# Gate and value products of a token-mixing MLP on one core: exchanging the stationary and the streamed operand

## The chip, the cores and the metric

One core of a Trainium2 chip runs the whole program in one launch. The metric is the device time in microseconds (us). Engines are named as in the profile: PE is TensorE, split into PE (the matmul streams) and PEld (the loads of the stationary operand), DVE is VectorE, ACT is ScalarE, POOL is GpSimd, SP is SyncE, whose queue issues the DMAs here.

## The reference, cut to what matters

Attention over 8 batches, 8 heads, 512 local and 32 global tokens makes x with 8 × 544 rows (tokens) of 512 columns. A two-layer MLP with a gate follows:

```python
xk = mu_k * x + (1.0 - mu_k) * x_prev
xr = mu_r * x + (1.0 - mu_r) * x_prev
k = np.maximum(xk @ w_k, 0.0)
v = k * k @ w_v
r = 1.0 / (1.0 + np.exp(-(xr @ w_r)))
return (r * v).astype(np.float32)
```

w_k is 512 × 1024, w_v 1024 × 512, w_r 512 × 512. The *keys* are `xk @ w_k`, the *gate* is r, the *values* are v. The output has 512 columns, called e below.

## The kernel before

**Tiling.** Tokens are worked in groups of 256 (`TOK`): two for each batch, and one for all global tokens, 17 in all. Features lie on the 128 partitions and tokens along the row. Each operand is split into a high part in the rounded 4-byte format that PE streams fast (`F32R`) and a low part, the rest, in the same format. A product is three matmuls: high × high, high × low, low × high (`products`, L615; `matmul`, L159, is the helper that every matmul passes through, so that its line in the profile is L160; transposes are L163).

**Gate** (`gates`, L706, and for the first batch `step_gates`, L1147, with `step_tanh`, L1154). For each 128-column block of w_r, 4 contraction blocks × 3 matmuls are made: the weight block is stationary, 256 tokens stream. Two such blocks fill one bank of PSUM. A token group has 4 blocks, so 48 matmuls of 256 columns. ACT then takes the tanh out of the bank (L717, L1158), and after the second bank one more ACT instruction maps the whole gate tile to 0.5 + 0.5·tanh (L719, L1160).

**Values.** The four token groups of batches 0 and 1 use plain products (`values`, L722, and `step_values`, L1162): 8 contraction blocks × 3 × 4 blocks = 96 matmuls of 256 columns for each group. DVE multiplies a finished bank into the gate tile and the result is stored (L731, `write` L741). Batches 2 to 7 and the global tokens use seven (or, for the global tokens, four) products of sums of blocks instead of eight (`Keys.product`, L820): the stationary operand is a 128-column piece of a sum of weight blocks (`left`, loaded from `scratch`), the streamed one is a sum of key blocks for 256 tokens (`right`, split by ACT and by DVE or POOL at L787 and L788). Halves of the outputs are summed by DVE and multiplied into the gate by POOL (`write`, L745), then stored.

**Output.** The gate tile is `[P, NC, TOK]`: features on partitions, blocks of e, then tokens; a half of the columns e is a contiguous half of a partition's row. The outputs are laid out as `(C, P, B, SL)` and `(C, P, B * SG)`, e first, and put in order on the host. A store (L916, L921) writes 1 KB runs of tokens.

**Order.** PE runs strictly in the order of the source (`in_line`, L149, chains every matmul to the one before). ACT, DVE and POOL keep the order of the source too. SP does so for the first stretch. That stretch (up to about 123 us) is written out by hand in `FIRST` (L66): steps such as `W.0.1` (gate, token group 0, part 1), `V.1.0` (values), `L.12` (low part of weight chunk 12 made by POOL). The eight chunks of w_v are loaded 12 to 19, chunk 12, that of contraction block 0, last. Later batches alternate attention steps and MLP steps by a pattern (`BATCH`, L1365); each `yield` in `gates` and `values` ends one MLP step. At `FILL_AT` (L1364) four small transposes are inserted into one gate.

```python
def products(out, w_h, w_l, cols, x_h, x_l, n):
    for i in range(n):
        matmul(out, w_h[:, i, cols], x_h(i), start=(i == 0), stop=False)
        matmul(out, w_h[:, i, cols], x_l(i), start=False, stop=False)
        matmul(out, w_l[:, i, cols], x_h(i), start=False, stop=(i == n - 1))
```

The first operand after `out` is the stationary one, the second is streamed.

Of the kernel before, what the change touches and what calls it, by code (L numbers as in the profile page):

```python
# [10 lines left out]
F32 = mybir.dt.float32  # L11
# [9 lines left out]
P = 128  # L21
D = 64
SG = 32
SL = 512
# [66 lines left out]
def local_global_attention_then_rwkv_ffn(  # L91
# [49 lines left out]
    def psum(tag):  # L141
        n = turn[tag] = turn.get(tag, -1) + 1
        pool = use[tag][n % len(use[tag])]
        return pool.tile([P, 512], F32, tag="ps", name=f"ps_{tag}")
# [473 lines left out]
            matmul(out, w_h[:, i, cols], x_l(i), start=False, stop=False)  # L618
            matmul(out, w_l[:, i, cols], x_h(i), start=False, stop=(i == n - 1))

    class Tokens:


# [81 lines left out]

        def gates(self, pool=None, fill_at=None):  # L706

            pool = pool or gatep
            self.gate = pool.tile([P, NC, TOK], F32, tag="gate", name="gate")
            for e0 in range(0, NC, 2):  # L710
                rp = psum("m").rearrange("p (j n) -> p j n", j=2)
                for j in range(2):
                    if (j, e0) == fill_at:
                        fill_narrow(rp[:, j], 4)
                    products(rp[:, j], wr_h, wr_l, slice((e0 + j) * P, (e0 + j + 1) * P),
                             lambda c: self.xr_h[:, c], lambda c: self.xr_l[:, c], NC)
                Tokens.square = nc.scalar.activation(self.gate[:, e0:e0 + 2], rp, AF.Tanh, scale=0.5)  # L717
                if e0 + 2 == NC:
                    nc.scalar.activation(self.gate, self.gate, AF.Copy, scale=0.5, bias=0.5)  # L719
                yield  # L720

        def values(self):  # L722
            for e0 in range(0, NC, 2):
                vp = psum("m").rearrange("p (j n) -> p j n", j=2)
                for j in range(2):
                    products(vp[:, j], wv_h, wv_l, slice((e0 + j) * P, (e0 + j + 1) * P),
                             lambda f: self.kk_h[f], lambda f: self.kk_l[f], NF)
                    if j == 0:
                        yield
                o = self.gate[:, e0:e0 + 2]  # L730
                nc.vector.tensor_mul(o, vp, o)  # L731
                self.store(slice(e0, e0 + 2), o)
                yield

        def write_one(self, e, v):

            o = self.gate[:, e]
            nc.vector.tensor_mul(o, v, o)
            self.store(slice(e, e + 1), self.gate[:, e:e + 1])

        def write(self, half, v):  # L741

            es = slice(2 * half, 2 * half + 2)
            o = self.gate[:, es]
            (nc.vector if v.tensor.name.startswith("ps_") else nc.gpsimd).tensor_mul(o, v, o)  # L745
            self.store(es, o)

    class Keys:

# [70 lines left out]
        def product(self, out, b, fresh=True, apart=False, between=None):  # L820
            right = self.parts.pop(b)
            steps = [(i, j) for i in range(HC) for j in range(2)]
            if between:
                steps.sort(key=lambda x: x[1])
            for i, j in steps:
                a, (b_h, b_l) = left[i // 2], right[i // 2]
                a_h, a_l = (a[:, i % 2, x, j * P:(j + 1) * P] for x in range(2))
                for n, (w, x) in enumerate(((a_h, b_h), (a_h, b_l), (a_l, b_h))):
                    matmul(
                        out[j] if apart else out[:, j], w, x[:, i % 2],  # L830
                        start=fresh and (i, n) == (0, 0) and (apart or j == 0),
                        stop=(i, n) == (HC - 1, 2), skip_group_check=True,
                    )
# [58 lines left out]
        def values_of_one(self):  # L892

            t, = self.tokens
            X, Y = self.bank(), [self.bank()[:, 0] for _ in range(2)]
            parts = [self.parts[f"B{b}1"] for b in (1, 2)]

            def product(out, b, **how):
                self.parts["end"] = parts[b]
                self.product(out, "end", fresh=not b, **how)  # L900
            product(X, 0)
            yield
            product(Y, 0, apart=True)
            yield
            product(X, 1)
            t.write(0, X)
            yield
            product(Y, 1, apart=True, between=lambda j: t.write_one(2 + j, Y[j]))
            yield


    def local_tokens(b, half, xT):
        at = half * TOK

        def store(es, o):
            nc.sync.dma_start(out=out_l[es, :, b, at:at + TOK].rearrange("e p n -> p e n"), in_=o)  # L916
        return Tokens(lambda c: xT[c][:, 1 + at:1 + at + TOK], lambda c: xT[c][:, at:at + TOK], lambda a: a, store)

    def global_tokens():
        def store(es, o):  # L920
            nc.sync.dma_start(out=out_g[es].rearrange("e p n -> p e n"), in_=o)  # L921
# [222 lines left out]
        kh, kl = squares_of(t, f)  # L1144
        nc.vector.tensor_sub(kl, banks["K", t, f], kh.bitcast(F32))

    def step_gates(t, e):  # L1147
        rp = banks["W", t, e] = psum("m").rearrange("p (j n) -> p j n", j=2)
        x_h, x_l = first[int(t)].part("r")
        for j in range(2):  # L1150
            at = (2 * int(e) + j) * P
            products(rp[:, j], wr_h, wr_l, slice(at, at + P), lambda c: x_h[:, c], lambda c: x_l[:, c], NC)

    def step_tanh(t, e):  # L1154
        t_, e0 = first[int(t)], 2 * int(e)
        if e0 == 0:
            t_.gate = gatep.tile([P, NC, TOK], F32, tag="gate", name="gate")
        nc.scalar.activation(t_.gate[:, e0:e0 + 2], banks["W", t, e], AF.Tanh, scale=0.5)  # L1158
        if e0 + 2 == NC:
            nc.scalar.activation(t_.gate, t_.gate, AF.Copy, scale=0.5, bias=0.5)  # L1160

    def step_values(e, j):  # L1162
        if j == "0":
            banks["V", e] = psum("m").rearrange("p (j n) -> p j n", j=2)
        at = (2 * int(e) + int(j)) * P
        products(banks["V", e][:, int(j)], wv_h, wv_l, slice(at, at + P),
                 lambda f: first[0].kk_h[f], lambda f: first[0].kk_l[f], NF)

    STEPS = {
        "@": step_load,  # L1170
# [31 lines left out]
        "W": step_gates,  # L1202
        "w": step_tanh,
        "V": step_values,
        "v": lambda e: first[0].write(int(e), banks["V", e]),
    }

    by_hand = ExitStack()
# [247 lines left out]
```

## Time and profile before

| | us |
|---|---|
| device time, median of 3 runs (lowest to highest) | 630.81 (630.70 to 631.17) |
| span of the profiled execution, first to last instruction | 628.5 |
| PE busy | 620.1 (99%) |
| PEld busy | 590.7 (94%) |
| DVE, ACT, POOL busy | 440.0, 379.7, 340.1 |

The page gives the profiled execution its span alone; the median of the runs is 2.3 us above that span. Matmuls are pipelined: a record opens before the array is free, so the pace of a run of matmuls is read from the distance between starts, or from a long run's length over its count, not from the duration of one. The chain of work that ended last is followed back from the last instruction, at each step to what released it; a stretch of it that lies on PE is one in which PE waited for nobody.

### The profile page before, as it was taken

The page shows a single profiled execution, that of the slowest core. Times are in us where ns is not written, and L with a number is a line of the kernel's source. Part 1 is how long each engine was busy: PE and PEld are TensorE (multiplying, and loading weights), DVE is VectorE, ACT ScalarE, POOL GpSimd, SP SyncE. Part 2 cuts the span into 40 slices and gives each one's busy share as a digit, 9 for nine tenths or more (in the row PEclk, how much of TensorE's full clock was granted, in tenths as well). Part 3 has the DMA queues.
Part 4 walks back from the last instruction along what each step waited for, and adds up shares of the span by engine and source line. Part 5 has one row for each costly group of instructions (what it writes and reads, how often), then busy time and mean ns, then how long its engine had stood idle before and what let it go on. Part 6 is the DMA issues. An engine that isn't in the chain of part 4 may idle for free.

```text
span 628.5 us, 20469 instructions
## 1 busy us (share of the span) xinstructions
PE 620.1 (99%) x8356; PEld 590.7 (94%) x8356; DVE 440.0 (70%) x1227; ACT 379.7 (60%) x1147; POOL 340.1 (54%) x310
## 2 busy tenths in 40 slices
PE   8999999999999999999999999999999999999997
PEld 4689999999999999999999999999999999999997
DVE  7999983758888487676695677676696657345960
ACT  6899967164383768565857657665847744433531
POOL 8786455536846245846276535846275534543660
PEclk9999999999999999999999999999999999999999
DMA  8955562457383546276463928276463834377684
GB/s 337 408 197 217 193 224 82 169 183 273 118 305 131 201 139 236 60 269 235 158 248 108 378 75 335 88 267 228 162 243 104 299 117 137 105 222 246 200 261 142
DMA packets 43278, 127.29 MB, mean 203 GB/s; under 512 B 3760, under 2 KB 20656, under 8 KB 43184
## 3 DMA queue, kind: packets, MB, share of 16 engines
q1 hardware_dynamic: 43184, 125.98, 56.1%
q8 instruction: 66, 1.08, 0.7%
q14 instruction: 28, 0.23, 0.1%
HBM read 108.66 MB, written 17.30 MB: 200 GB/s over the span
## 4 chain that ended last, share of the span: by engine, by line
PE 85%; DVE 5%; DMA 3%; POOL 3%; ACT 2%; issue 1%; DVEq 0%; POOLq 0%; ACTq 0%
PE ps_m L160 65%; PE ps_s L160 13%; PE ps_t L163 4%; PE ps_t L160 2%; DMA w<-w_v 2%; ACT Pt L417 1%; PE ps_s L163 1%; DMA raw_qk<-qk 1%; POOL wv_l L271 1%; DVE a L299 1%; DVE diff L664 1%; POOL w L252 1%; POOL Pt L428 0%; DVE diff L659 0%; DVE xfull L664 0%
## 5 line engine op out<-in xcount | busy, mean ns | idle before, releaser
L160 PE MATMUL ps_m<-xkh,wk_h 128*128 128x256 f32 x544 | 154.1, 283 | 0.0
L160 PE MATMUL ps_m<-xkl,wk_h 128*128 128x256 f32 x544 | 150.5, 277 | 0.0
L160 PE MATMUL ps_m<-xkh,wk_l 128*128 128x256 f32 x544 | 150.5, 277 | 0.0
L160 PE MATMUL ps_m<-bh,a 128*128 128x256 f32 x736 | 131.7, 278 | 0.0
L428 POOL TENSOR_TENSOR Pt<-Pt,ssum 128x512 f32<-128x512 f32 x64 | 69.4, 1088 | 81.0 <-ACT Pt L417 38.9
L160 PEld LDWEIGHTS ps_m<-bh,a 128*128 128x128 f32 x736 | 113.1, 188 | 0.0
L417 ACT ACTIVATE Pt<-Pt,m 128x128 f32<-128x128 f32 x256 | 99.5, 395 | 14.4 <-DVE m L410 14.4
L160 PEld LDWEIGHTS ps_m<-xkh,wk_h 128*128 128x128 f32 x544 | 102.2, 188 | 3.7 <-issue 1.2
L160 PEld LDWEIGHTS ps_m<-xkh,wk_l 128*128 128x128 f32 x544 | 102.3, 188 | 0.0
L160 PEld LDWEIGHTS ps_m<-xkl,wk_h 128*128 128x128 f32 x544 | 102.2, 188 | 0.0
L160 PE MATMUL ps_m<-bl,a 128*128 128x256 f32 x368 | 101.7, 276 | 0.0
L160 PE MATMUL ps_m<-xrh,wr_h 128*128 128x256 f32 x272 | 76.7, 282 | 0.0
L702 ACT ACTIVATE relu<-ps_m 128x512 f32<-128x512 f32 x52 | 30.9, 595 | 74.3 <-PE ps_m L160 69.0
L669 POOL TENSOR_TENSOR xkl<-xfull,xkh 128x512 fp32r<-128x512 f32 x30 | 40.2, 1339 | 65.8 <-DVE ssum L361 33.6
L160 PE MATMUL ps_m<-xrl,wr_h 128*128 128x256 f32 x272 | 75.2, 277 | 0.0
L160 PE MATMUL ps_m<-xrh,wr_l 128*128 128x256 f32 x272 | 75.2, 276 | 0.0
L410 DVE CUSTOM_DVE_ANT_0 Pt<-ps_s,masks 128x128 f32<-128x128 f32 x256 | 55.9, 285 | 24.2 <-PE ps_s L160 24.2
L160 PEld LDWEIGHTS ps_m<-bl,a 128*128 128x128 f32 x368 | 69.2, 188 | 0.0
L669 POOL TENSOR_TENSOR xrl<-diff,xrh 128x512 fp32r<-128x512 f32 x30 | 41.5, 1383 | 41.8 <-DVE xrh L668 26.7
L788 DVE TENSOR_TENSOR bl<-B,bh 128x512 fp32r<-128x512 f32 x41 | 40.1, 992 | 27.6 <-ACT bh L787 27.4
L788 POOL TENSOR_TENSOR bl<-B,bh 128x512 fp32r<-128x512 f32 x35 | 47.8, 1387 | 19.1 <-ACT bh L787 11.4
L664 DVE SCALAR_TENSOR_TENSOR diff<-diff,mu_r_sb,xT 128x256 f32<-128x256 f32 x56 | 57.2, 1061 | 0.0
(154 smaller groups left out, 1477.3 us busy)
## 6 DMA issues: line engine op xcount, KB each, us to landing
a<-scratch SPq DMA_DIRECT2D x92, 512.0 KB, 4.8
raw_v<-v SPq DMA_DIRECT2D x32, 896.0 KB, 8.6
raw_qk<-qk SPq DMA_DIRECT2D x32, 628.0 KB, 5.0
out_l<-gate SPq DMA_DIRECT2D x32, 256.0 KB, 2.2
w<-w_k SPq DMA_DIRECT2D x8, 512.0 KB, 12.9
w<-w_v SPq DMA_DIRECT2D x8, 512.0 KB, 4.0
w<-w_r SPq DMA_DIRECT2D x4, 512.0 KB, 3.6
scratch<-wv_h SPq DMA_DIRECT2D x8, 256.0 KB, 2.7
```

The source lines that it names most:

```text
L160: return in_line(nc.tensor.matmul(*a, **kw))
L163: return in_line(nc.tensor.transpose(*a, **kw))
L252: nc.gpsimd.tensor_scalar(word(n, F32, 1), word(n, F32, 1), REBIAS, 1.0, op0=ALU.mult, op1=ALU.mult)
L271: nc.gpsimd.tensor_sub(part_of_weights(n, "l"), word(n, F32, 0), part_of_weights(n, "h").bitcast(F32))
L299: nc.vector.tensor_sub(s.bitcast(F32R), s, hs.bitcast(F32))
L410: nc.vector.tensor_tensor_reduce(out=self.Pt[:, i], in0=self.place(t, n, h), in1=masks[:, 2 * self.slots[t][1] + n], op0=ALU.add, op1=ALU. ...
L417: nc.scalar.activation(self.Pt[:, i], self.Pt[:, i], AF.Exp, bias=self.low_x[:, i:i + 1], scale=-1.0, accum_out=self.ssum[:, i:i + 1],)
L428: nc.gpsimd.tensor_mul(self.Pt[:, some], self.Pt[:, some], inv.unsqueeze(2).to_broadcast([P, 4, W]))
L664: nc.vector.scalar_tensor_tensor(self.shape(xf[:, j]), self.shape(d[:, j]), mu[:, c0 + j:c0 + j + 1], self.prev(c0 + j), op0=ALU.mult, op1 ...
L669: nc.gpsimd.tensor_sub(lo[:, both], xf, hi[:, both].bitcast(F32))
L702: nc.scalar.activation(rk, kp, AF.Relu)
L788: (by or (nc.vector if b[0] == "B" else nc.gpsimd)).tensor_sub(l, val, h.bitcast(F32))
```

## The change

Gate and plain value products put a block of 128 tokens in as the stationary operand and stream 512 weight columns past it. The blocked value products of batches 2 to 7 exchange their operands too and stay 256 columns wide. The result has tokens on partitions, so the gate tile is `[P, 2, NC * P]` (128 tokens, two token blocks, 512 columns e) and the outputs are `(B, SL, C * P)` and `(B * SG, C * P)`; a half of the columns e is now two pieces of 256 in a partition's row.

```diff
+    def by_tokens(out, x_h, x_l, j, w_h, w_l, part, n):
+        rows = slice(j * P, (j + 1) * P)
+        for i in part:
+            matmul(out, x_h(i)[:, rows], w_h[:, i], start=(i == 0), stop=False)
+            matmul(out, x_l(i)[:, rows], w_h[:, i], start=False, stop=False)
+            matmul(out, x_h(i)[:, rows], w_l[:, i], start=False, stop=(i == n - 1))
...
         def gates(self, pool=None, fill_at=None):
-            self.gate = pool.tile([P, NC, TOK], F32, tag="gate", name="gate")
-            for e0 in range(0, NC, 2):
-                rp = psum("m").rearrange("p (j n) -> p j n", j=2)
-                for j in range(2):
-                    if (j, e0) == fill_at:
-                        fill_narrow(rp[:, j], 4)
-                    products(rp[:, j], wr_h, wr_l, slice((e0 + j) * P, (e0 + j + 1) * P),
-                             lambda c: self.xr_h[:, c], lambda c: self.xr_l[:, c], NC)
-                Tokens.square = nc.scalar.activation(self.gate[:, e0:e0 + 2], rp, AF.Tanh, scale=0.5)
-                if e0 + 2 == NC:
+            self.new_gate(pool or gatep)
+            for j in range(2):
+                rp = psum("m")
+                if j == fill_at:
+                    fill_narrow(rp, 4)
+                self.gate_of(j, rp)
+                Tokens.square = nc.scalar.activation(self.gate[:, j], rp, AF.Tanh, scale=0.5)
+                if j:
                     nc.scalar.activation(self.gate, self.gate, AF.Copy, scale=0.5, bias=0.5)
                 yield
...
+        def new_gate(self, pool):
+            self.gate = pool.tile([P, 2, NC * P], F32, tag="gate", name="gate")
+        def gate_of(self, j, bank):
+            by_tokens(bank, lambda c: self.xr_h[:, c], lambda c: self.xr_l[:, c], j, wr_h, wr_l, range(NC), NC)
+        def values_part(self, j, half, bank):
+            part = range(half * NF // 2, (half + 1) * NF // 2)
+            by_tokens(bank, lambda f: self.kk_h[f], lambda f: self.kk_l[f], j, wv_h, wv_l, part, NF)
         def values(self):
...
+            for j in range(2):
+                vp = psum("m")
+                self.values_part(j, 0, vp)
                 yield
+                self.values_part(j, 1, vp)
+                self.write_rows(j, vp)
+                yield
+        def write_rows(self, j, v, es=slice(0, NC * P)):
+            o = self.gate[:, j, es]
             nc.vector.tensor_mul(o, v, o)
+            self.store(slice(j, j + 1), es, self.gate[:, j:j + 1, es])
         def write(self, half, v):
-            es = slice(2 * half, 2 * half + 2)
-            o = self.gate[:, es]
+            es = slice(half * TOK, (half + 1) * TOK)
+            o = self.gate[:, :, es]
             (nc.vector if v.tensor.name.startswith("ps_") else nc.gpsimd).tensor_mul(o, v, o)
-            self.store(es, o)
+            self.store(slice(0, 2), es, o)
...
                 a, (b_h, b_l) = left[i // 2], right[i // 2]
-                a_h, a_l = (a[:, i % 2, x, j * P:(j + 1) * P] for x in range(2))
-                for n, (w, x) in enumerate(((a_h, b_h), (a_h, b_l), (a_l, b_h))):
+                a_h, a_l = (a[:, i % 2, x] for x in range(2))
+                rows = slice(j * P, (j + 1) * P)
+                for n, (x, w) in enumerate(((b_h, a_h), (b_l, a_h), (b_h, a_l))):
                     matmul(
-                        out[j] if apart else out[:, j], w, x[:, i % 2],
+                        out[j] if apart else out[:, j], x[:, i % 2, rows], w,
...
-            product(Y, 1, apart=True, between=lambda j: t.write_one(2 + j, Y[j]))
+            product(Y, 1, apart=True, between=lambda j: t.write_rows(j, Y[j], slice(TOK, 2 * TOK)))
...
-            nc.sync.dma_start(out=out_l[es, :, b, at:at + TOK].rearrange("e p n -> p e n"), in_=o)
+            nc.sync.dma_start(out=out_l[b, at:at + TOK].rearrange("(j p) e -> p j e", p=P)[:, js, es], in_=o)
...
-    FILL_AT = {(B - 2, 1): (1, 0)}
+    FILL_AT = {(B - 2, 1): 0}
...
-    outs = {"out_l": (C, P, B, SL), "out_g": (C, P, B * SG)}
+    outs = {"out_l": (B, SL, C * P), "out_g": (B * SG, C * P)}
```

`step_gates`, `step_tanh` and `step_values` of the first stretch are rewritten to the same calls; the text of `FIRST` is unchanged, so that `V.1.0` now means token block 1, contraction blocks 0 to 3.

## Rows read from the trace of the kernel before

**Rows 1.** The page: span, busy time of each engine.
```profile
span 628.5 us, 20469 instructions
PE 620.1 (99%) x8356; PEld 590.7 (94%) x8356; DVE 440.0 (70%) x1227; ACT 379.7 (60%) x1147; POOL 340.1 (54%) x310
```
**Rows 2.** Chain that ended last, 523 us to the end: start us, us, what, count.
```profile
523.21 102.03 PE ps_m L160 x900
```
**Rows 3.** Busy time of PE, PEld, DVE, ACT, POOL in two stretches, then clock and DMA.
```profile
141.70:171.60 29.90, 29.64 (x371) 29.02 (x370) 25.73 (x43) 10.88 (x28) 22.18 (x19) 1.00 0.57 201
...
220.00:523.00 303.00, 303.00 (x4247) 293.61 (x4247) 213.04 (x603) 197.26 (x589) 163.88 (x127) 1.00 0.55 198
```
**Rows 4.** Groups by line and shape, PE and PEld: shape, count, busy us, mean ns, idle before.
```profile
L160 PE MATMUL ps_m<-bh,a 128*128 128x256 f32 x736 | 131.7, 278 | 0.0
L160 PE MATMUL ps_m<-xrh,wr_h 128*128 128x256 f32 x272 | 76.7, 282 | 0.0
L160 PE MATMUL ps_m<-kkh,wv_h 128*128 128x256 f32 x128 | 36.8, 287 | 0.0
...
L160 PEld LDWEIGHTS ps_m<-xrh,wr_h 128*128 128x128 f32 x272 | 51.1, 188 | 1.1
L160 PEld LDWEIGHTS ps_m<-xT,diag 128*128 128x128 f32 x32 | 5.7, 189 | 0.9 <-ACT xT L611 0.2
```
**Rows 5.** Chain that ended last, 87 to 117 us.
```profile
87.77 6.38 DMA w<-w_v
...
99.38 10.94 PE ps_m L160 x94
...
110.76 2.83 PE ps_m L160 x24
...
114.03 2.74 PE ps_m L160 x24
```
**Rows 6.** PE in order of time at 99 and 171 us: waits in brackets.
```profile
99.38 0.39 PE L160 MATMUL ps_m<-kkh,wv_l 128*128 128x256 f32 x1 [0.39 <-POOL wv_l L271]
...
171.60 0.62 PE L160 MATMUL ps_s<-raw_qk 128*64 128x480 f32 x2 [0.26 <-DVE m L410]
```
**Rows 7.** Chain that ended last, 143 to 171 us.
```profile
143.05 0.44 DVE kkh L682
...
169.50 1.11 DVE kkl L683
```
**Rows 8.** Chain that ended last, 213 to 221 us.
```profile
213.34 0.61 ACT relu L702
...
219.96 0.63 PE ps_t L163 x4
```
**Rows 9.** Matmuls with the high part of w_r in two stretches: PE busy us, count.
```profile
141.50:171.60 30.10, 5.49 (x32) 1.00 0.57 202
...
219.90:628.50 408.60, 70.20 (x400) 1.00 0.55 195
```
**Rows 10.** PEld in order of time, fp32 loads (xT, diag): first and last of three.
```profile
26.90 0.19 PEld L160 LDWEIGHTS ps_m<-xT,diag 128*128 128x128 f32 x1
...
27.33 0.19 PEld L160 LDWEIGHTS ps_m<-xT,diag 128*128 128x128 f32 x1
```
**Rows 11.** PE in order of time, fp32 matmuls of 256 columns (xT, diag) at 26 us.
```profile
26.36 0.48 PE L160 MATMUL ps_m<-xT,diag 128*128 128x256 f32 x1
26.68 0.38 PE L160 MATMUL ps_m<-xT,diag 128*128 128x256 f32 x1
```
**Rows 12.** The page's DMA issues: stores, KB each, median us to landing.
```profile
out_l<-gate SPq DMA_DIRECT2D x32, 256.0 KB, 2.2
```
**Rows 13.** POOL and DVE in order of time, multiplications into the gate tile.
```profile
289.04 1.67 POOL L745 TENSOR_TENSOR gate<-sum,gate 128x512 f32<-128x512 f32 x1 [0.15 <-DVE sum L879]
295.37 1.67 POOL L745 TENSOR_TENSOR gate<-sum,gate 128x512 f32<-128x512 f32 x1 [0.44 <-DVE sum L888]
622.60 0.69 DVE L745 TENSOR_TENSOR gate<-ps_m,gate 128x512 f32<-128x512 f32 x1 [12.02 <-issue]
```

More of the change, by code (lines that the diff above doesn't have):

```diff
@@ L706, in gates @@
         def gates(self, pool=None, fill_at=None):
-            pool = pool or gatep
-            self.gate = pool.tile([P, NC, TOK], F32, tag="gate", name="gate")
-            for e0 in range(0, NC, 2):
-                rp = psum("m").rearrange("p (j n) -> p j n", j=2)
-                for j in range(2):
-                    if (j, e0) == fill_at:
-                        fill_narrow(rp[:, j], 4)
-                    products(rp[:, j], wr_h, wr_l, slice((e0 + j) * P, (e0 + j + 1) * P),
-                             lambda c: self.xr_h[:, c], lambda c: self.xr_l[:, c], NC)
-                Tokens.square = nc.scalar.activation(self.gate[:, e0:e0 + 2], rp, AF.Tanh, scale=0.5)
-                if e0 + 2 == NC:
+            self.new_gate(pool or gatep)
@@ L719, in gates @@
+            for j in range(2):
[5 more added lines that the diff above has]
+                if j:
                     nc.scalar.activation(self.gate, self.gate, AF.Copy, scale=0.5, bias=0.5)
                 yield
-        def values(self):
[L723 to L732, printed above, removed]
-                yield
@@ L735, in write_one @@
-        def write_one(self, e, v):
-            o = self.gate[:, e]
+        def new_gate(self, pool):
[5 more added lines that the diff above has]
+            by_tokens(bank, lambda f: self.kk_h[f], lambda f: self.kk_l[f], j, wv_h, wv_l, part, NF)
@@ L738, in write_one @@
+        def values(self):
+            for j in range(2):
+                vp = psum("m")
+                self.values_part(j, 0, vp)
+                yield
+                self.values_part(j, 1, vp)
[3 more added lines that the diff above has]
+            o = self.gate[:, j, es]
             nc.vector.tensor_mul(o, v, o)
-            self.store(slice(e, e + 1), self.gate[:, e:e + 1])
+            self.store(slice(j, j + 1), es, self.gate[:, j:j + 1, es])
@@ L913, in local_tokens, with store @@
         at = half * TOK
-        def store(es, o):
-            nc.sync.dma_start(out=out_l[es, :, b, at:at + TOK].rearrange("e p n -> p e n"), in_=o)
+        def store(js, es, o):
+            nc.sync.dma_start(out=out_l[b, at:at + TOK].rearrange("(j p) e -> p j e", p=P)[:, js, es], in_=o)
         return Tokens(lambda c: xT[c][:, 1 + at:1 + at + TOK], lambda c: xT[c][:, at:at + TOK], lambda a: a, store)
     def global_tokens():
-        def store(es, o):
-            nc.sync.dma_start(out=out_g[es].rearrange("e p n -> p e n"), in_=o)
+        def store(js, es, o):
+            nc.sync.dma_start(out=out_g.rearrange("(j p) e -> p j e", p=P)[:, js, es], in_=o)
         return Tokens(lambda c: xg_all[:, c, :, 1:SG + 1], lambda c: xg_all[:, c, :, 0:SG],
@@ L1145, in step_squares_low, with step_gates, step_tanh, step_values @@
         nc.vector.tensor_sub(kl, banks["K", t, f], kh.bitcast(F32))
[L1147 to L1159, printed above, removed]
-            nc.scalar.activation(t_.gate, t_.gate, AF.Copy, scale=0.5, bias=0.5)
[L1162 to L1167, printed above, removed]
+    def step_gates(t, j):
+        banks["W", t, j] = psum("m")
+        first[int(t)].gate_of(int(j), banks["W", t, j])
+    def step_tanh(t, j):
+        t_ = first[int(t)]
+        if j == "0":
+            t_.new_gate(gatep)
+        nc.scalar.activation(t_.gate[:, int(j)], banks["W", t, j], AF.Tanh, scale=0.5)
+        if j == "1":
+            nc.scalar.activation(t_.gate, t_.gate, AF.Copy, scale=0.5, bias=0.5)
+    def step_values(j, half):
+        if half == "0":
+            banks["V", j] = psum("m")
+        first[0].values_part(int(j), int(half), banks["V", j])
     STEPS = {
@@ L1204, in local_global_attention_then_rwkv_ffn @@
         "V": step_values,
-        "v": lambda e: first[0].write(int(e), banks["V", e]),
+        "v": lambda j: first[0].write_rows(int(j), banks["V", j]),
     }
@@ L1452 @@
     res = run_bass_kernel_spmd(nc, [arrays], core_ids=[0]).results[0]
-    o_l = res["out_l"].reshape(C * P, B, SL).transpose(1, 2, 0)
-    o_g = res["out_g"].reshape(C * P, B, SG).transpose(1, 2, 0)
+    o_l = res["out_l"].reshape(B, SL, C * P)
+    o_g = res["out_g"].reshape(B, SG, C * P)
     return np.ascontiguousarray(np.concatenate([o_g, o_l], axis=1))
```

## The prediction, made before the changed kernel ran

> **What bounds the kernel now.** I read the page first: PE is busy for 620.1 of 628.5 us and DVE, the next engine, for 440.0 [rows 1]. A pipelined PE that is busy is not yet PE at its peak, so the chain of waits comes next: where it lies on PE, nobody keeps PE waiting, and an instruction fewer there is time gained. Its last long piece is one run of 900 matmuls without a wait, 102.03 us [rows 2]; 102.03 / 900 = 113.4 ns for each. At 2.4 GHz, the granted clock (1.00 in both stretches of [rows 3]), 256 columns are 106.7 ns, so each matmul pays 6.7 ns above its columns. That is what the change can reach: the columns stay the same, the matmuls become half as many.
>
> How many? The gate has three forms of 272 matmuls, 816 = 17 token groups × 48; the plain values have three of 128, 384 = 4 groups × 96 [rows 4]. All 1200 are 256 wide and become 600 of 512: **600 pairs**. The blocked products, 736 with a high right-hand part [rows 4] and, as one matmul in three takes the low part, half as many with a low one, stay 256 wide.
>
> Then I ask where the chain is not on PE, because a pair there gives nothing. Up to 99.4 us it runs through the loads of w_v [rows 5] and what POOL makes of them, for which PE waits [rows 6]. From 143 to 171 us it runs through DVE: the first and the last row of that piece are [rows 7], DVE is busy for 25.73 of the 29.90 us there [rows 3], and PE stands for 0.26 us behind it at the end [rows 6]. From 213.3 to 220.0 us it runs through ACT [rows 8]. From 220 to 523 us PE is busy for all 303.00 us, with DVE at 213 and ACT at 197 [rows 3], and the run of 900 follows. How many pairs a stretch holds is counted by the matmuls that read the high part of w_r, two in three: 32 of them are a whole gate, so 24 pairs, and 400 are 300 pairs [rows 9].
>
> **What one pair is worth.** No matmul of this fast format with 512 columns is in the trace. The nearest rows are the fp32 ones of xT and diag: 256 columns at two clock cycles each, so 512 cycles of streaming, with a stationary load as long as the gate's (189 against 188 ns, [rows 4]). Their loads stand 0.43 us apart over two steps [rows 10], 215 ns each; I take 216. So a pair goes from 2 × 113.4 = 226.8 to 216: **10.8 ns**. My reading is that at 256 columns the 128-column load sets the pace, since it is hidden beneath too short a stream, and at 512 it no longer does. The bounds: if the whole 6.7 ns is a cost of each matmul whatever its width, a pair gives 6.7; if 512 columns take their bare 213.3 ns, 13.5; if the 6.7 ns goes with the columns, 0. I take 216, since those rows have the same cycles and the same load.
>
> The rule that speaks against this is in the Trainium skill, "TensorE: Matmul & The Clock Gate", section "Back-to-back issue gap": the gap is the columns over the clock plus about 2.5 ns, 109.2 ns for 256. By it a pair would give 2.5 ns, the pairs that count in the sum below 1.2 us, and the time would be 629.6. The trace does not agree at this width: it shows 113.4.
>
> In the plain values the pace is worse than 113.4: 24 matmuls take 2.83 or 2.74 us by turns [rows 5], 116 ns in the mean. If the long stream hides that too, a pair gives 2 × 116 − 216 = 16 ns.
>
> **The sum by stretches.**
> - To 99.4 us: the first batch's gate, 48 pairs. The chain is with the loads, so 0. If that cover were gone, 0.5 us.
> - 99.4 to 110.3 us: the first 96 value matmuls. Two run ahead, then PE waits 0.39 us for POOL [rows 6]; 94 follow in 10.94 us [rows 5], 10.8 without the last one's drain. Afterwards the two that run ahead are long ones and still fit before 99.4, so 46 follow: 9.94. Gain 0.83.
> - 110.5 to 123 us: the other group, 48 pairs × 16 ns = 0.77.
> - 143 to 171 us: one gate (24 pairs, [rows 9]) and one group of values (48). DVE's chain does not get shorter; PE's wait of 0.26 us grows by what PE gains, some 1.0 us. Counted 0. What is late next there is DVE itself.
> - 171.6 to 213 us: 24 × 10.8 ns + 48 × 16 ns = 1.03.
> - 213 to 220 us: half a gate, 12 pairs, behind ACT: 0.
> - 220 us to the end: half a gate and twelve whole ones [rows 9], 300 pairs × 10.8 ns = 3.24.
>
> Pairs: 48 + 48 + 48 + 72 + 72 + 12 + 300 = 600. **Gain 0.83 + 0.77 + 1.03 + 3.24 = 5.87 us.** The profiled span of 628.5 would become 622.6; the median of the runs lies 2.3 above that span before, and with the same 2.3 it becomes 624.9.
>
> **The edits that I cost at nothing.** The blocked products keep their 1104 matmuls, their width and a load for each; the operands change places. A right-hand part, made late by DVE or POOL, must now be there for the load, about one matmul (0.113 us) sooner. No idle time is put down to these matmuls today [rows 4], so that much earlier costs nothing where the part is ready; bounds 0 and 0.113 us for a part that comes just in time. Tanh, scaling and multiplications keep their counts and sizes. Stores: a half of the columns is 1 KB runs as before, the plain values get 2 KB runs; they land in 2.2 us [rows 12] and only the last is on the path. The four filling transposes move ahead of their gate by twelve matmuls, with the same work. Half as much of a gate's or value's contraction is needed in the first 2.7 us of it, so operands may come later than today; bound from below a gain that I leave out. Last, the halves of a gate tile are now interleaved. If the second half's multiplication is made to wait for the first half's store, POOL stands, and with it the parts that it makes for the next product. In mid-batch the two lie 295.37 − 289.04 = 6.3 us apart, 1.67 of it the first multiplication and 2.2 the store [rows 12, 13]: 2.4 us to spare. At the end the first half is multiplied at 622.60 [rows 13], so its store lands about 625.5, and the two last multiplications would come up to 0.7 us late. Ends 0 and 0.7; I take 0, since the two halves of a tile show no such wait today [rows 13].
>
> **The rivals.**
> - *A fixed cost for each matmul*, 6.7 ns at any width: 467 pairs outside the covered stretches × 6.7 ns = 3.1 us, **627.7**. For it: a constant step above the bare columns is all that the run of 900 shows. Against: 215 ns for 512 cycles is 1.7 above them, not 6.7 [rows 10].
> - *Nothing is covered*: the stretches that I set to 0 shorten too, because DVE, ACT and the loads start from earlier PE work. 0.52 + 1.03 + 0.13 = 1.7 us more, **623.2**. Against: those pieces are filled end to end by the other engine [rows 3, 7].
> - *The extra goes with the columns*: the fast format streams at 1.06 cycles a column, and 512 take 224.8 to 226.8 ns. Gain 0 to 0.9 us, **629.9 to 630.8**, no change. The rule of the Trainium skill above comes to the same verdict by its 2.5 ns.
> - *Slower: exposed loads.* The stationary operand is now written just ahead by ACT, DVE and POOL instead of lying ready for long. If its load is held back until the stream before it has ended, it is not hidden. The first of the xT, diag run shows the price: 26.36 to 26.68 is 320 ns [rows 11], 105 more than 215. Above 5.87 / 0.105 = 56 such loads the kernel is slower. If every blocked product pays it for each of its four fresh tiles ((736 + 368) / 24 = 46 products, 184 loads), it is 19.3 us, **644.2**. Against: the gate's streamed parts are just as fresh today, and the pace is even.
>
> **How the numbers follow.** My forecast, 624.9, has 0.66: its own range is 623.7 (512 columns at the bare 213.3) to 627.0 (half of what the uncovered pairs give beyond 6.7 ns each, and the last 0.7 us). Fixed cost 0.10, nothing covered 0.09, with the columns 0.09, exposed loads 0.06. A measurement of this kernel tells about 0.2% (1.26 us) from no change. Faster by more: 0.66 + 0.10 + 0.09 = 0.85. Same: 0.09. Slower: 0.06. The range takes in the forecast, the fixed cost and the covers that don't hold: 623.0 to 628.0, which leaves out 0.15.
>
> **What would show it.** Right: 600 gate and value matmuls of 512 columns 215 to 217 ns apart; PE and PEld at 8356 − 600 = 7756 instructions each; PEld some 600 × 0.188 = 113 us less busy; the last run of matmuls about 1.0 us shorter (180 gate matmuls in it become 90); the wait of 0.39 us for POOL at 99 us shorter, that for DVE near 170 us about 1 us longer. Wrong: a pace of 220 (fixed cost) or 225 (with the columns); stretches before 99, from 143 to 171 or 213 to 220 us that end earlier relative to their start; waits in front of the loads of blocked products; POOL idle behind stores.

## The result, and the profile after

The changed kernel takes **635.3 us** (median of 4 runs, 634.29 to 636.35), the kernel before, run beside it, 630.99 (630.70 to 631.25). The ratio is 1.0064, interval 1.0050 to 1.0079: slower by 0.64%, where 624.9 and a gain were forecast.

First the page of the changed kernel: its span, its engines and the shares of the engines in its chain; then its groups by form (columns as in [rows 4]).

```profile
span 633.8 us, 19271 instructions
...
PE 626.1 (99%) x7756; PEld 569.5 (90%) x7756; DVE 441.8 (70%) x1227; ACT 379.9 (60%) x1147; POOL 340.3 (54%) x310
...
PE 95%; ACT 2%; DMA 1%; DVE 1%; issue 0%; POOL 0%; ACTq 0%
```

```profile
L160 PE MATMUL ps_m<-a,bh 128*128 128x256 f32 x736 | 135.1, 280 | 0.0
...
L160 PE MATMUL ps_m<-wr_h,xrh 128*128 128x512 f32 x136 | 54.6, 402 | 0.0
...
L160 PE MATMUL ps_m<-wv_h,kkh 128*128 128x512 f32 x64 | 26.3, 411 | 0.0
```

The 600 matmuls are gone (8356 in [rows 1], 7756 here), and PE is nevertheless busy for 6.0 us longer. Nothing new makes it wait: the chain lies on PE for 95% (85% before). The work itself has become slower. Where, the chain of waits shows (start us, us, what, count). The changed kernel from 213 us on:

```profile
213.39 0.61 ACT relu L710
...
220.01 0.63 PE ps_t L163 x4
...
491.09 5.72 PE ps_m L160 x24
...
497.68 5.66 PE ps_m L160 x48
...
504.21 5.66 PE ps_m L160 x48
...
525.05 0.59 PE ps_m L163 x4
525.63 104.86 PE ps_m L160 x816
```

The same places of the kernel before:

```profile
487.66 5.66 PE ps_m L160 x48
...
494.19 5.46 PE ps_m L160 x48
...
500.52 5.45 PE ps_m L160 x48
...
521.16 1.61 PE ps_m L160 x12
```

At 220 us the two kernels are level (219.96 before [rows 8], 220.01 after). The last stretch begins at 521.16 before and at 525.05 after, so 3.84 us are lost between; it ends at 523.21 + 102.03 = 625.24 [rows 2] against 525.63 + 104.86 = 630.49, another 1.36. The three pieces of one batch tell what they consist of. A gate has half as many matmuls and takes 5.72 instead of 5.66 us. And each of the two pieces behind it, a pair of blocked products (24 matmuls each) **with the same 48 matmuls of the same width**, takes 5.66 instead of 5.46: 118 ns a matmul instead of 113.6.

The stretches of busy time of one tile's own instructions say the same of the whole span. First the blocked products (all that read `a`), then two thirds of the keys (all that read `wk_h`); columns as in [rows 3], the second number is PE. Before:

```profile
0.00:640.00 640.00, 131.68 (x1104) 127.64 (x1104) 11.01 (x8) 25.73 (x24) 1.00 0.56 199
...
0.00:640.00 640.00, 191.92 (x1088) 164.07 (x1088) 5.39 (x8) 10.31 (x8) 1.00 0.56 199
```

After:

```profile
0.00:640.00 640.00, 135.12 (x1104) 131.40 (x1104) 11.01 (x8) 25.75 (x24) 1.00 0.56 199
...
0.00:640.00 640.00, 193.80 (x1088) 164.71 (x1088) 5.37 (x8) 10.31 (x8) 1.00 0.56 199
```

If each matmul but the last is charged with the time to the next one's start, over the whole trace, the sums close: blocked products 126.7 before and 130.1 after, keys 190.9 and 192.9, gates 95.2 and 95.8, plain values 46.1 and 45.3, everything else 164.3 and 164.3. The difference is 5.2 us; the profiled spans differ by 5.3, the medians by 4.3. The part that was to gain is worth 0.63 − 0.80 = −0.2 us; the loss is in 256-wide products that the change leaves as many and as wide as they were.

**Two paces.** Seen start by start, such a run goes at 113.3 ns or at 117.8 ns a matmul, and keeps to one of them from its first few matmuls to its last. In the fifteen whole kernels three runs change in between. One is in the kernel before: within a blocked product that ran at 113.3, a step takes 178 ns, and the rest of the product goes on at 118 (columns as in [rows 6]).

```profile
256.33 0.34 PE L160 MATMUL ps_m<-bl,a 128*128 128x256 f32 x1
256.51 0.40 PE L160 MATMUL ps_m<-bh,a 128*128 128x256 f32 x2
```

I count by half groups, 12 matmuls in line. At the slower pace are, before: 1 of 92 half groups of blocked products, 10 of 136 of keys, 12 of 32 of values, 3 of 68 of gates. After: 70 of 92 and 46 of 136. All 56 half groups of blocked products of batches 2 to 5 are among them; the other 36, of batches 6 and 7 and of the global tokens, belong to the last 105 us. At 4.45 ns a matmul, 69 more half groups of blocked products and 36 more of keys would cost 3.7 and 1.9 us; the sums above give 3.4 and 2.0.

### The profile page after: what moved, and what is told of

Read it like the earlier page. It is cut to its first block, busy times and chain, and to the rows that moved or that the text cites. A ratio compares the mean times of both kernels' runs of the same rounds, so it can differ in the third digit from the quotient of the medians.

```text
span 633.8 us, 19271 instructions
## 1 busy us (share of the span) xinstructions
PE 626.1 (99%) x7756; PEld 569.5 (90%) x7756; DVE 441.8 (70%) x1227; ACT 379.9 (60%) x1147; POOL 340.3 (54%) x310
## 4 chain that ended last, share of the span: by engine, by line
PE 95%; ACT 2%; DMA 1%; DVE 1%; issue 0%; POOL 0%; ACTq 0%
PE ps_m L160 73%; PE ps_s L160 15%; PE ps_t L163 5%; PE ps_t L160 2%; ACT Pt L417 1%; PE ps_s L163 1%; DMA raw_qk<-qk 1%; POOL Pt L428 0%; DVE Pt L410 0%; ACT relu L710 0%; ACT PT L456 0%; ACT Pg L509 0%; POOL Pg L515 0%; ACT B L711 0%; DVE ps_m L260 0%
## 5 line engine op out<-in xcount | busy, mean ns | idle before, releaser
L160 PE MATMUL ps_m<-a,bh 128*128 128x256 f32 x736 | 135.1, 280 | 0.0
L160 PEld LDWEIGHTS ps_m<-a,bh 128*128 128x128 f32 x736 | 114.2, 188 | 0.2
L160 PE MATMUL ps_m<-a,bl 128*128 128x256 f32 x368 | 102.5, 279 | 0.0
L160 PEld LDWEIGHTS ps_m<-a,bl 128*128 128x128 f32 x368 | 69.2, 188 | 0.3
L160 PEld LDWEIGHTS ps_s<-PT,raw_v 128*64 128x64 f32 x1568 | 50.0, 138 | 6.5 <-issue 3.2
L160 PE MATMUL ps_m<-wr_h,xrh 128*128 128x512 f32 x136 | 54.6, 402 | 0.0
L160 PE MATMUL ps_m<-wr_l,xrh 128*128 128x512 f32 x136 | 53.5, 394 | 0.0
```

The costliest lines, as they stand in the source:

```text
L160: return in_line(nc.tensor.matmul(*a, **kw))
```

## The experiments

By *apart* I mean the address of the streamed operand less that of the stationary one, in bytes, modulo 512, from the programs' layouts. Blocked products before: 448; after: 64, since the operands have changed places. Keys: 192 in both. Where one orientation of the products meets the other in the gate tile (runs 1, 2, 8, 10, 11 and 13), part of the output is not the layer's, and the work is the same.

**Which part of the change?** Run 1 puts the operands of `product` back, run 2 is the kernel before with only these exchanged, run 3 is the changed kernel with each 512-wide matmul as two of 256.

```diff
-                for n, (x, w) in enumerate(((b_h, a_h), (b_l, a_h), (b_h, a_l))):
+                for n, (w, x) in enumerate(((a_h, b_h), (a_h, b_l), (a_l, b_h))):
```

> The changed kernel (635.3) with the operands of the blocked products put back: weight sums stationary, key sums streamed; gate and plain values stay 512 wide. Inside each block of a blocked product rows and columns come out exchanged, so those outputs are not the reference's. Theory 'exchange' (token blocks as stationary operand of the blocked products set their pace to 118 ns instead of 113): they return to 113.3, the key products beside them too, and the time is 630 to 632.3. Theory 'neighbour' (512-wide streams leave the 256-wide ones behind them in a slow pace): blocked products stay at 117 to 118 and the time is 634.5 to 636. In both the 512-wide matmuls stay near 229 ns.

> The kernel before (631.0) with the operands of the blocked products exchanged and nothing else; gate and plain values stay 256 wide with weights stationary. Inside each block of a blocked product rows and columns come out exchanged. Theory 'exchange': blocked products at 117 to 118 ns, 1104 x 3 to 4.5 ns = 3.5 to 5 us, 634 to 636. Theory 'neighbour': they stay at 113.3 and the time is 630.5 to 631.5.

> The changed kernel with each 512-wide matmul made as two of 256, each with its own load of the token block: 7756 + 600 matmuls. Theory 'columns' (the fast format streams 16 columns in 17 cycles, and a 512-wide matmul pays 2.4 ns on top where a 256-wide one pays none): gate and values at 113.3, 600 x 2.3 = 1.4 us less, 633.5 to 634.5. If the exchange itself slows 256-wide matmuls to 118 wherever it is made: 1200 x 4.5 = 5.4 us more than that, 637 to 640. If the long stream was worth its 10.8 ns a pair and only the blocked products cost: 635.3 + 5 = 640 with the gate at 113.3.

Measured: run 1 635.0 (ratio 1.0056, 1.0039 to 1.0073), run 2 635.8 (1.0070, 1.0042 to 1.0097), run 3 639.2 (1.0120, 1.0096 to 1.0144). Each half of the change alone costs as much as both. In run 2 the exchange alone puts the 56 half groups at 118. In run 1 they are at 118 as well, though these products are untouched:

```profile
455.64 5.71 PE ps_m L160 x24
...
462.23 5.66 PE ps_m L160 x48
```

Run 3 shows that the width itself is no loss against the same products in two halves: 64 of 68 half groups of gates fall to 118, and the median is 3.9 us above the changed kernel's. The time lies where it was put for an exchange that slows 256-wide matmuls wherever it is made; run 8 below, with 63 of its 92 exchanged half groups at 113.3, speaks against that.

**What is the pace made of?** A kernel with matmuls alone, in runs of 48, at many widths and places; its output is zeros.

> No part of the reference is computed: one core runs groups of 48 matmuls of the fast format with four transposes between them and stores zeros. First widths 128 to 512 in steps of 64 columns, then 256 and 512 columns with only 64 stationary columns, then 256 and 512 columns with the address of the streamed or of the stationary operand moved in steps of 32 bytes. Theory 'columns': pace 17/16 of columns over 2.4 GHz, 113.3 at 256, 170 at 384, 226.7 (to 229) at 512, and the same with 64 stationary columns. Theory of the prediction (the load of 128 columns sets the pace at 256): 113 at 128, 192 and 256, 162 at 384, 216 at 512, and 109 at 256 with 64 stationary columns. Theory 'addresses' (the relative place of the two operands decides whether a 256-wide run goes at 113 or at 118): the pace changes between these two with the offset. Theory 'history' (only what ran before decides): the pace is the same at every offset.

In order of time, nine of its runs (start us, us with the last one's drain, form, count):

```profile
13.12 5.56 PE L58 MATMUL bank<-moving,still 128*128 128x128 f32 x48
...
18.89 5.59 PE L58 MATMUL bank<-moving,still 128*128 128x192 f32 x48
...
24.67 5.99 PE L58 MATMUL bank<-moving,still 128*128 128x256 f32 x48
...
30.85 7.29 PE L58 MATMUL bank<-moving,still 128*128 128x320 f32 x48
...
38.33 8.59 PE L58 MATMUL bank<-moving,still 128*128 128x384 f32 x48
...
47.12 9.98 PE L58 MATMUL bank<-moving,still 128*128 128x448 f32 x48
...
57.29 11.16 PE L58 MATMUL bank<-moving,still 128*128 128x512 f32 x48
...
68.64 5.71 PE L58 MATMUL bank<-moving,still 128*64 128x256 f32 x48
...
74.54 11.29 PE L58 MATMUL bank<-moving,still 128*64 128x512 f32 x48
```

128 and 192 columns go at one pace, 111.7 ns by the starts: there the load of 128 columns sets it. (The third such kernel, below, has 128-wide matmuls with both loads: they start 109 to 114 ns apart with 128 columns of load and 59 to 64 with 64.) At 256 the load does not: with half the load (64 columns) the pace is 113.5. That is a single run; whether a slower pace occurs with half the load too was not tried. 512 columns went at 226.65 ns at best, twice 113.3, and at 229.8 with half the load. So this fast format streams some 17 cycles for 16 columns (256 × 17/16 / 2.4 GHz = 113.3, an estimate that fits these two widths), and a longer stream wins nothing. The widths between fit it less well: 146.7 ns at 320 columns, 173.3 at 384 and 202.7 at 448 are 3 to 5 ns above it. By the place of the operands, one run for each, 512 columns ranged from 226.65 to 234.3, and 229 at 64 apart, the gate's place in the changed kernel. At 256, 2 of the 31 places ran at 113.4 to 113.7 and the rest between 116.7 and 120. That made the place the first suspect.

**Is it the place?** Run 4 is the changed kernel with a pad that brings the blocked products back to 448 apart; run 5 also moves the gate weights to 256 apart; run 6 is the kernel before with the pad alone, which brings it to 64.

```diff
+            place("shift_a", 1).tile([P, 32], F32, name="shift_a")
             leftp, sump, gate3 = (
...
+            gatew.tile([P, 48], F32, name="shift_r")
             wr_h, wr_l = (gatew.tile([P, NC, NC * P], F32R, name=f"wr_{x}") for x in "hl")
```

> The changed kernel with a pad of 128 bytes on every partition ahead of the tiles of the left sides, so that streamed and stationary operand of the blocked products stand 448 bytes apart (modulo 512) again, as before the change, instead of 64. Theory 1, the place of the operands in memory sets the pace: mid-batch blocked products go back to 113.3 ns, some 3.7 us come back and part of the 1.9 us of the key products behind them: 630.0 to 632.0. Theory 2, the 512-wide matmuls in front put the engine into the slow pace, whatever the addresses: no change, 634.5 to 636. Theory 3, what is streamed and what is loaded (the roles as such) sets it: no change either, 634.5 to 636; the run with no exchange (635.0) speaks against it already.

> As the run before it, and a pad of 192 bytes ahead of the gate weights, so that they stand 256 bytes from the stationary tokens instead of 64. Theory 1: the 408 gate matmuls of 512 columns go from 229.0 to 226.7 ns, 0.9 us less than the run before it: 629.2 to 631.2. Theories 2 and 3: the gate matmuls may do that too, but the blocked products stay at 118: 633.5 to 635.5.

> The kernel before with the pad of 128 bytes alone: its blocked products, with their old roles, get operands 64 bytes apart instead of 448. Theory 1: they run at 118 instead of 113.3, 1104 by 4.5 ns is up to 5.0 us, and key products behind them may follow: 633.5 to 637. Theories 2 and 3: no 512-wide matmul and no exchange, so nothing changes: 630.7 to 631.7.

Run 6 is the clearest run of this study: no instruction is changed, only left sides, sums and one gate tile lie 128 bytes lower, and it takes 634.3 (ratio 1.0042, 1.0029 to 1.0055). All 56 half groups are at 118; one pair of its blocked products, and the whole of them:

```profile
462.60 5.66 PE ps_m L160 x48
```

```profile
0.00:640.00 640.00, 134.31 (x1104) 130.16 (x1104) 11.02 (x8) 25.74 (x24) 1.00 0.57 199
```

But even there the place does not decide alone: the 36 half groups of the last 105 us stand 64 apart as well, and all of them run at 113.3. And the reverse fails. Run 4 took 634.4 (1.0043, 1.0029 to 1.0057): in each of batches 2 to 5 four of the seven blocked products returned to 113.3, three stayed at 118. Run 5 took 635.7 (1.0064, 1.0051 to 1.0076): its gates run at 227 instead of 229 ns, as expected of the place, and all 56 half groups are at 118 although they stand at 448. (Runs 4 and 5 restore the difference of the addresses, not the addresses; run 1 has the very addresses of the kernel before, and its 56 are at 118 too.) So 64 apart goes with the slower pace in batches 2 to 5, though not in the last stretch, and 448 is not enough for the faster.

**Is it what ran in front?** Two more kernels of matmuls alone. The first has six pairs of places, each behind transposes, behind 512-wide matmuls and behind an idle stretch; the second has three pairs, each behind 16 leads.

> Runs of 36 matmuls of 256 columns alone, without the rest of the kernel, at six pairs of operand places (those of the kernels among them), each behind four transposes, behind twelve 512-wide matmuls and behind an idle stretch, in two orders, and then a chain of runs without anything between. Its output is not the attention layer's. Theory 1: the pace goes by the pair alone, 113.3 at 448/0, 448/256 and 384/448, near 118 at 0/448, the same behind each predecessor. Theory 2: the pace goes by what ran in front, slow behind the 512-wide ones at every pair.

> Runs of 24 matmuls of 256 columns alone, at three pairs of operand places, each behind four or five transposes and behind a lead of one to three other matmuls: widths of 64 to 512 columns, or loads of 32 to 96 columns. Its output is not the attention layer's. Theory 4, a run keeps whichever of two paces it fell into at its entry, and a few ns there decide: behind one and the same lead some pairs run at 113.3 and some at 118, and a run that was slow without a lead is fast behind some lead. Theory 1, the pair of places decides: the column of a pair is the same behind all leads. What is open: whether one lead brings all six of its runs to 113.3.

From the chain of the first: the pair 448/256 (streamed/stationary address modulo 512) behind four transposes in the first and in the second order, then 384/448 likewise.

```profile
18.46 4.10 PE bank L63 x36
...
130.35 4.25 PE bank L63 x36
```

```profile
27.69 4.24 PE bank L63 x36
...
121.14 4.10 PE bank L63 x36
```

4.10 / 36 = 113.9 and 4.25 / 36 = 118: **one pair behind one kind of predecessor takes either pace**, and 384/448 the other way round. Over the 36 runs 6 of 12 are at 113.3 behind transposes, 4 of 12 behind 512-wide matmuls, 7 of 12 behind idleness: the predecessor does not decide either. In the second kernel the places bias the draw: 448/0 is at 113.3 in 20 of 32 runs, 448/256 in 23, 0/448 (64 apart) in 4. No lead brings all six of its runs to 113.3; three leads bring five, one 512-wide matmul among them. At the entry the two are told apart by a few ns: of all the runs in the kernels before, after and 1 to 6 that begin behind a product of attention weights and values, 54 of 57 with a first step of 220 to 224 ns went on at 113.3, and all 22 with 225 or more at 118. But 4.5 ns is also what one step at the slower pace adds, so the longer first step may be its first sign and not its cause.

**The draw in the whole kernel.** Run 7 is the changed kernel at 192 apart, run 9 the kernel before at 192. Run 8 has the exchanged blocked products alone, at 192; runs 10 and 11 the wide gates and values alone, with the gate weights moved by 192 bytes and with the left sides at 192; run 12 is the changed kernel with one more transpose ahead of its blocked products.

```diff
             steps = [(i, j) for i in range(HC) for j in range(2)]
+            if fresh and not apart:
+                fill_narrow(out[:, 0], 1)
```

> The changed kernel with a pad of 384 bytes ahead of the left sides: streamed and stationary operand of the blocked products 192 bytes apart, as those of the key products, which run at 113.3 in their long runs. Theory 1: all blocked products at 113.3, 630.5 to 632. Theory 4: another draw at each entry, some at 113.3 and some at 118: 632.5 to 636, and the time follows the number of matmuls at 118, 4.4 ns each.

> The kernel before with a pad of 256 bytes ahead of the left sides, 192 bytes between the blocked products' operands. Theory 1: as before, 630.7 to 632. Theory 4: a new draw; the kernel before has 26 of 328 half groups at 118, so a new one will rather have more: 632 to 636.

> The kernel before with the exchanged blocked products alone (gates and values stay 256 wide), and a pad of 384 bytes, which puts their operands 192 bytes apart; without the pad, 64 apart, that kernel took 635.8. If the exchange costs only by the places (theory 1 for this part): blocked products at 113.3 as in the two kernels before with 448 and 192 bytes, 631 to 632. If the roles themselves do it: over half of the blocked products at 118 again, 634.5 to 636.

> The 512-wide gates and values alone (blocked products as before the change), with a pad of 192 bytes ahead of the gate weights: 512-wide gates at 227 instead of 229 ns, 0.6 to 0.9 us. Without the pad that kernel took 635.0, its mid-batch blocked products at 118 though their operands stand as in the kernel before. If what counts is the few ns with which the gates end in front (theory 4), the blocked products can come out at either pace: 630.5 (all at 113.3) to 634.5.

> The 512-wide gates and values alone, with the blocked products' operands 192 bytes apart instead of 448, the pad that left the kernel before as it was. If the wide matmuls in front spoil the blocked products at every place (theory 2): mid-batch ones at 118 again, 634 to 636. Theory 4: either pace by entry, 630.8 to 635.

> The changed kernel with one more 128-column transpose of the identity ahead of each blocked product with a bank of its own (some 22, of about 0.11 us each, 2.4 us in all); addresses, roles and gates as in the changed kernel. Theory 4: some of the blocked products that ran at 118 run at 113.3 and some of those at 113.3 at 118, 632 to 639. Theories 1, 2 and 3: the same runs stay at 118, 637 to 638.5.

Half groups at 118, all runs (blocked products of batches 2 to 5, those of the last 105 us, keys), and the ratio to the kernel before. The counts are of one execution of each kernel; whether another one draws the same was not tried.

| kernel | gates, values wide | blocked exchanged | apart | of 56 | of 36 | keys, of 136 | us | ratio (interval) |
|---|---|---|---|---|---|---|---|---|
| before | no | no | 448 | 1 | 0 | 10 | 631.0 | 1 |
| 9 | no | no | 192 | 1 | 0 | 28 | 631.5 | 0.9996 (0.9987 to 1.0005) |
| 6 | no | no | 64 | 56 | 0 | 32 | 634.3 | 1.0042 (1.0029 to 1.0055) |
| 2 | no | yes | 64 | 56 | 18 | 32 | 635.8 | 1.0070 (1.0042 to 1.0097) |
| 3 | in two halves | yes | 64 | 56 | 28 | 44 | 639.2 | 1.0120 (1.0096 to 1.0144) |
| 8 | no | yes | 192 | 23 | 6 | 62 | 635.5 | 1.0063 (1.0050 to 1.0077) |
| 1 | yes | no | 448 | 56 | 0 | 28 | 635.0 | 1.0056 (1.0039 to 1.0073) |
| 11 | yes | no | 192 | 56 | 0 | 32 | 634.8 | 1.0050 (1.0035 to 1.0064) |
| 10 | yes, at 256 | no | 448 | 0 | 36 | 86 | 636.3 | 1.0074 (1.0057 to 1.0091) |
| after | yes | yes | 64 | 56 | 14 | 46 | 635.3 | 1.0064 (1.0050 to 1.0079) |
| 4 | yes | yes | 448 | 24 | 18 | 50 | 634.4 | 1.0043 (1.0029 to 1.0057) |
| 7 | yes | yes | 192 | 24 | 18 | 54 | 635.5 | 1.0060 (1.0049 to 1.0072) |
| 5 | yes, at 256 | yes | 448 | 56 | 18 | 62 | 635.7 | 1.0064 (1.0051 to 1.0076) |
| 12 | yes | yes | 64 | 56 | 32 | 46 | 641.3 | 1.0155 (1.0140 to 1.0170) |
| 13 | values only | no | 448 | 0 | 0 | 36 | 631.3 | 0.9990 (0.9981 to 0.9999) |

(Run 13 is told below.) With old roles and narrow gates the place alone tells the 56 half groups (kernel before, 9 and 6). With wide gates or exchanged operands it does not: at 448 or 192 apart the count is anything from 0 (run 10) to 56 (runs 1, 5 and 11).

Against what was expected, run 9 (631.5) stayed as fast as theory 1 has it and did not get the 632 or more of a redraw, though more of its keys are at 118. Runs 7 and 8 (635.5) miss theory 1, which had 632 at most; run 7 fits the redraw of theory 4. Run 8 has the time of *the roles themselves*, but not by their means: 29 of its 92 half groups of blocked products are at 118, not over half, and its keys lose more (2.7 us) than its blocked products (1.7). Run 11 (634.8) fits theory 2 and theory 4 alike; theory 2, the wide matmuls in front, falls with run 10, which at 636.3 lies beyond theory 4's 634.5 as well.

Run 10 is the plainest against every simple rule: the wide gates stand in front, and all 56 are at 113.3; but the 36 of the last stretch and most of the keys have gone to 118, and the whole is as slow as ever. Its chain, gate and two pairs of blocked products, and its keys:

```profile
488.70 5.67 PE ps_m L160 x24
...
495.25 5.47 PE ps_m L160 x48
...
501.59 5.46 PE ps_m L160 x48
```

```profile
0.00:640.00 640.00, 195.73 (x1088) 165.71 (x1088) 5.41 (x8) 10.35 (x8) 1.00 0.56 199
```

Run 12 missed its figure of 637 to 638.5 for an unmoved pace, and went past the redraw's too. There were 37 transposes (7793 matmuls against 7756), not 22: 4.1 us at 0.11 each. Blocked products of the last stretch went to 118 besides (32 of 36, 14 without the transposes): 18 × 12 × 4.45 ns = 1.0 us. The profiled spans differ by 5.2 (639.0 and 633.8). The 56 did not move: 64 apart, they are at 118 in all five kernels that have them there (after, 2, 3, 6, 12). A pair of its products, each now with a transpose ahead:

```profile
500.12 0.11 PE ps_m L163
500.23 2.83 PE ps_m L160 x24
503.06 0.11 PE ps_m L163
503.17 2.83 PE ps_m L160 x24
```

**The wide values alone.** The kernel before with `by_tokens` for the plain values of batches 0 and 1, and nothing else.

> The kernel before with the 512-wide values of the first two batches alone; gates, keys and blocked products as they were. The values it writes for those batches stand turned against their gates. If an entry's pace goes by what is in the SBUF and just in front of it, the runs of batches 2 to 7 keep theirs (blocked products at 113.3) and only the values change: 12 of 32 half groups leave 118 and all go to 114.5 a pair half, 46.1 to 45.3 us: 630.3 to 631.5. If any edit, however far ahead, redraws the entries behind it, some of the mid-batch blocked products go to 118: 632 to 636.

Measured 631.3 against 631.9 beside it, ratio 0.9990 (0.9981 to 0.9999). This is the gaining part of the change, about as small as can be told. Its values go from 46.1 to 45.3 us by the starts, and no blocked product is at 118 (span, all blocked products, two thirds of the keys):

```profile
span 628.7 us, 20085 instructions
```

```profile
0.00:640.00 640.00, 131.64 (x1104) 127.61 (x1104) 11.03 (x8) 25.77 (x24) 1.00 0.56 199
...
0.00:640.00 640.00, 193.19 (x1088) 164.48 (x1088) 5.62 (x8) 10.45 (x8) 1.00 0.56 199
```

So the edit does not spoil the blocked products from afar. It does not leave everything behind it alone, though: 36 half groups of keys are at 118 instead of 10, sixteen of them (2 before) behind 222 us, in batches whose matmuls were not touched. They cost 1.3 us, so that the profiled execution (628.7) is no shorter than that of the kernel before (628.5), and the expectation that only the values would change failed for the keys. What run 1 has beyond this kernel is the wide gates; they bring its blocked products to 118, and at another place (run 10) they do not. Run 13 is the quickest kernel of the study, by a tenth of a per cent, but not a complete one: its gates would have to be turned for those batches alone, which was not tried.

## Why the prediction was wrong

*What bounds the kernel* held: PE's own pace is the time, and the chain stays on PE. The counts held too: 600 matmuls fewer, 300 pairs behind 220 us. PEld was to be 113 us less busy and is so by 21 (590.7 to 569.5): 600 durations of 0.188 us were added up (their sum did fall by 112), but records of loads overlap.

*What one pair is worth* failed, and with it the forecast. The step took 216 ns for 512 columns from fp32 rows "with the same cycles and the same load". They have other cycles: the fast format's 512 columns take 226.7 ns at best and 229 at the gate's place. A pair gives −2.3 ns, not 10.8, and lies beyond the lower bound of 0, which had named 226.8 as the worst. The reading behind it, that the 128-column load sets the pace at 256, is refuted by the half load (113.5, one run). Of the rivals, *the extra goes with the columns* was the true one for this step. By the 2.5 ns rule of the Trainium skill ("TensorE: Matmul & The Clock Gate", section "Back-to-back issue gap"), which is given there for the isolated gap, 512 columns would be an estimated 215.8 ns; here they are not under 226.65, and the measurement decides. The same section says that the spacing in a stream of loads and matmuls is set by both; 111.7 ns at 128 and at 192 columns agree with that.

*The plain values* were to gain 16 ns a pair; 192 pairs gained 0.80 us, 4 ns each, and not by a shorter stream: 12 of their 32 half groups had been at 118, and PE's wait at 99 us went. "The four groups pay 116 in the mean" was two paces mixed.

*The covers.* The wait for POOL at 99 us is gone, as foretold in direction. PE's wait near 170 us was to grow by 1.0 and has gone as well. The stretch behind ACT did not move. With no gain in the pairs none of this shows at 220 us.

*The edits that I cost at nothing* failed worst, with bounds of 0 and 0.113 us. The exchange of the blocked products' operands alone costs 0.70% (run 2). It adds no wait and no instruction; it puts the same matmuls at another pace. The loss of 5.2 us is 3.45 in blocked products, 1.94 in keys, 0.63 in gates, less 0.80 in values. The *exposed loads* of the slower rival did not occur: the first step of a run is longer before and after alike, and idle time stays at nothing in the groups. So that rival had the right sign by luck: the loss came from a mechanism that no rival names.

Shown: the loss is in runs at 118; moving operands by 128 bytes alone brings such a loss about (run 6); either half of the change does (runs 1 and 2); one pair takes either pace (the kernels of matmuls alone). Not settled: what decides a run's pace. The place biases it, an edit of what runs in front moves it (run 1 against run 13), and no rule in these runs foretells a kernel's draw. Why the kernel before has so few at 118 was not tried either.

## What to carry to other kernels

Before a change is costed by a pace, look at the starts of single runs: a mean of 116 ns can be two paces of 113 and 118, and an edit that leaves count, width and load alone can still move runs from the one to the other. Take the price of a wider matmul from the same data format, or measure it alone. A tuned kernel in which nearly all runs have the faster pace has some per mille to lose by almost any edit, a pad of 128 bytes included (here by twelve of fourteen; runs 9 and 13 are the two that cost nothing), so run such a pad as a control before a small gain or loss is put down to the idea.

## What was not expected of the hardware

Runs of 256-column matmuls in the 4-byte fast format, each with its own 128-column load, have two steady paces at a granted clock of 1.00: 113.3 and 117.8 ns, 4% apart, held for 36 matmuls and more. In the first kernel of matmuls alone the slower runs lay between 116.7 and 120. At 512 columns the pace goes from 226.65 to 234.3 ns with the places of the two operands in memory; the gates of the whole kernels agree at two places, 229 at 64 apart and 227 at 256 apart (runs 5 and 10).
